# Four edits ahead of the feed-forward part of a spectral block: a shorter chain to the first angles, gathers behind the last rstd, shared PSUM tiles for the last stage-1 casts, another order of the first pairs

## Chip, cores, metric

One core of one Trainium2 chip. The metric is the device time of one execution in microseconds (us), median of several runs. The profile gives in addition the span, from the first to the last instruction of the core (some 1.8 us less than the time).

## What is computed

```python
def reference(A_x, A_w_r, A_w_i, B_x, B_w1, B_b1, B_w2, B_b2):
    # x: (1, 2048, 512) bf16; w_r, w_i: (2048, 257); w1: (512, 1792); w2: (1792, 512)
    x = A_x
    h  = x + irfft2(rfft2(layernorm(x)) * (w_r + 1j * w_i))
    h2 = h + (relu(layernorm(h) @ w1 + b1) ** 2) @ w2 + b2
    return h2
```

The two-dimensional Fourier transforms are done as matmuls with tables of sines and cosines, which the kernel makes itself from integer angles. The 2048 rows are split into 16 groups of 128 for the first part.

## The kernel before: the parts concerned

The rows of x arrive in five loads. The third of them holds groups 4 to 7:

```python
CH = ((0, 2), (2, 4), (4, 8), (8, 12), (12, 16))
for a, b in CH:
    ld.append(nc.sync.dma_start(xs[:, a:b, :], xv[:, a:b, :]))
```

VectorE makes the first angles (fiE) out of the partition number, and then starts on the statistics of the layer norm:

```python
nc.vector.tensor_single_scalar(pI[:, 1:2], pI[:, 0:1], 3, ALU.arith_shift_right)
nc.vector.tensor_single_scalar(pI[:, 2:3], pI[:, 0:1], 7, ALU.bitwise_and)
nc.vector.tensor_copy(pF[:], pI[:, 0:3])
nc.vector.tensor_scalar(cols[:, 2:3], pF[:, 2:3], 512.0, None, ALU.mult)
nc.vector.tensor_scalar(cols[:, 3:4], pF[:, 1:2], 32.0, cols[:, 2:3], ALU.mult, ALU.add)
nc.vector.tensor_scalar(cols[:, 6:7], cols[:, 3:4], 16.0, None, ALU.mult)
nc.vector.tensor_scalar(ck1[:], idx1[:], cols[:, 3:4], None, ALU.mult)
nc.vector.scalar_tensor_tensor(fiE[0]..., idx2..., cols[:, 6:7], ck1..., ALU.mult, ALU.add)
```

Stage 1 multiplies two row groups at a time. The layer norm's rstd (one over the standard deviation of a row) is "folded" into the table (KFr = KF times rstd), TensorE multiplies, and the result in PSUM is cast to Bt. PSUM is one pool of four slots of two banks each (`bufs=4`, 1024 floats). The last four groups are "split": each half of a result has a slot of its own, so that ScalarE casts one half and VectorE the other:

```python
def stage1(g0, n=0, split=False, ...):
    if split:
        two = [mm_tile("p1a"), mm_tile("p1b")]
        pts = [pt[:, 0:512] for pt in two]
    else:
        pt = mm_tile("p1")
        pts = [pt[:, 0:512], pt[:, 512:1024]]
    ...                                     # 8 matmuls
    if split:
        for t, cph in ((0, nc.scalar.copy), (1, nc.vector.tensor_copy)):
            cph(dst[:, 2 * t:2 * t + 2], pts[t]...)
```

Then come eight pairs of frequencies. For each, stage 2 gives U, stage 3 gives A and B (AB, cast by ScalarE), VectorE makes X out of AB and multiplies X by the weights (mA, mB), combines them into Z and M, and stage 4 transforms back:

```python
stage2_one(0, 0, nc.vector.tensor_copy, 3)
stage2_one(0, 1, nc.scalar.copy)
stage2_one(1, 0, nc.scalar.copy)
...
stage3(0)
stage2_one(1, 1, nc.scalar.copy)
stage2(2)
stage3(1)
stage3(2)
for pr in range(9):
    ...                                     # stage 2 and 3 of later pairs, stage 4 of the last one
    spectral(pr)                            # VectorE
```

The weights of the rows above the middle are gathered by GpSimd, half of them before the last rstd, which GpSimd makes too.

## Time and profile before

| | before |
|---|---|
| time, median of 3 runs | 172.66 us (172.52 to 172.68) |
| span of the profile | 170.8 us |
| busy in the span: TensorE, VectorE, ScalarE, GpSimd | 92%, 72%, 62%, 22% |
| first angles (fiE) start | 2.48 |
| last two folds start | 17.47 |
| first multiply by the weights (mA) starts | 23.62 |
| last M of the spectral part ends | 48.00 |
| from there to the end of the span | 122.8 |

The last five rows are positions in us from the start of the span, read off VectorE's timeline. Everything that was edited lies before 48.0. TensorE's 92% is mostly the feed-forward part behind that point. The question is therefore not who is busiest but what sets the pace in each stretch of the first 48 us.

### The profile page before, as it was taken

How to read it: one execution, taken by the hardware profiler on the slowest of the kernel's cores; microseconds unless marked ns; L12 is line 12 of the kernel's file. 1: busy time of each engine (PE TensorE's matmuls, PEld its weight loads, DVE VectorE, ACT ScalarE, POOL GpSimd, SP SyncE). 2: the span in 40 equal slices, each digit the busy share in tenths (PEclk: the TensorE clock that was granted, in tenths of full speed). 3: DMA queues.
4: the chain of work that ended last, by engine and by line, in shares of the span. 5: the costliest groups of instructions: out<-in, count | busy, mean ns of one | idle time of the engine just before them, and what ended most of it. 6: DMA issues, size and time to landing. Idle time of an engine off the chain costs nothing.

```text
span 170.8 us, 2709 instructions
## 1 busy us (share of the span) xinstructions
PE 157.6 (92%) x967; PEld 92.4 (54%) x981; DVE 123.6 (72%) x287; ACT 106.3 (62%) x188; POOL 36.7 (22%) x63
## 2 busy tenths in 40 slices
PE   3988797999989899899999999999999999999992
PEld 1455565887854774456445444544544454556461
DVE  6998678979956698668997577498567577578320
ACT  3999785898976772288653677245387434478200
POOL 7788900000000003134000235000034200025000
PEclk9999999999999999999999999999999999999999
DMA  5994999992000000100000100000100001010011
GB/s 165 326 281 83 223 152 272 387 241 26 0 0 0 4 0 2 55 12 0 0 31 31 35 0 2 0 31 31 35 30 0 0 31 33 25 38 0 0 60 34
DMA packets 12621, 11.42 MB, mean 67 GB/s; under 512 B 6976, under 2 KB 11072, under 8 KB 12608
## 3 DMA queue, kind: packets, MB, share of 16 engines
q1 hardware_dynamic: 12448, 10.33, 22.6%
q0 software_dynamic: 160, 0.92, 1.9%
q8 instruction: 7, 0.11, 0.3%
q14 instruction: 6, 0.05, 0.1%
HBM read 8.01 MB, written 2.10 MB: 59 GB/s over the span
## 4 chain that ended last, share of the span: by engine, by line
PE 72%; DVE 16%; ACT 5%; issue 2%; POOL 2%; DVEq 0%; POOLq 0%; ACTq 0%
PE ph L688 29%; PE po L721 25%; DVE st L215 3%; PE p L542 3%; PE p L344 3%; ACT U L361 2%; PE po L709 2%; PE p L643 2%; PE p L587 1%; PE idle L259 1%; POOL rs L222 1%; DVE KFr L226 1%; DVE mA L419 1%; ACT X L391 1%; DVE mB L419 1%
## 5 line engine op out<-in xcount | busy, mean ns | idle before, releaser
L688 PE MATMUL ph<-UT,W 128*128 128x384 bf16 (+2 forms) x278 | 49.8, 336 | 1.6 <-DVE UT L774 0.6
L691 ACT ACTIVATE rl<-ph,b1f 128x384 bf16<-128x384 f32 (+2 forms) x70 | 41.5, 602 | 13.7 <-PE ph L688 10.6
L721 PE MATMUL po<-W,act 128*128 128x512 bf16 x203 | 48.1, 379 | 0.4
L692 DVE TENSOR_TENSOR act<-rl 128x384 bf16<-128x384 bf16 (+2 forms) x70 | 34.2, 514 | 15.4 <-ACT rl L691 14.9
L688 PEld LDWEIGHTS <-W 128*128 128x128 bf16 x280 | 27.3, 98 | 22.9 <-issue 2.1
L695 POOL TENSOR_TENSOR hb<-hs,b2b 128x512 f32<-128x512 bf16 x16 | 18.4, 1153 | 98.2 <-DVE act L692 98.2
L721 PEld LDWEIGHTS <-act 128*128 128x128 bf16 x210 | 20.4, 98 | 21.8
L725 DVE TENSOR_TENSOR ot<-po,hb 128x512 bf16<-128x512 f32 x15 | 10.3, 688 | 9.3 <-PE po L721 8.0
L591 DVE SCALAR_TENSOR_TENSOR hs<-p,xs 128x512 bf16<-128x512 f32 x15 | 10.3, 684 | 1.2 <-PE p L587 0.9
L259 PE MATMUL p<-ones 128*128 128x512 bf16 x22 | 8.1, 516 | 2.9 <-POOL ones L152 2.9
L546 ACT COPY od<-p 128x256 f32<-128x256 f32 x14 | 5.1, 370 | 7.9 <-PE p L542 7.9
L647 ACT COPY UT<-p 128x768 bf16<-128x768 bf16 (+1 forms) x4 | 3.6, 906 | 9.4 <-PE p L643 9.4
L542 PE MATMUL p<-GI,T 128*128 128x256 bf16 x56 | 8.2, 272 | 0.4 <-DVE hs L591 0.2
L259 PEld LDWEIGHTS <-ones 128*128 128x128 bf16 x40 | 4.4, 112 | 7.6 <-POOL ones L152 2.9
L602 ACT ACTIVATE junk<-hs 128x512 bf16<-128x512 bf16 x6 | 3.8, 630 | 7.6 <-DVE hs L591 7.6
L344 PE MATMUL p<-GF,Bt 128*128 128x256 bf16 x64 | 8.3, 273 | 0.0
L577 DVE TENSOR_TENSOR R<-p,od 128x256 bf16<-128x256 f32 x15 | 6.2, 415 | 2.4 <-ACT od L561 1.3
L215 DVE BATCH_NORM_STATS2 st<-xs 128x6 f32<-128x512 bf16 x12 | 7.8, 676 | 0.0
L542 PEld LDWEIGHTS <-T 128*128 128x128 bf16 x56 | 5.4, 97 | 3.5 <-issue 1.2
L473 ACT CAST T<-p 128x1024 bf16<-128x1024 f32 x7 | 7.2, 1025 | 0.0
L344 PEld LDWEIGHTS <-Bt 128*128 128x128 bf16 x64 | 6.1, 98 | 1.4 <-DVE Bt L251 0.4
L605 DVE BATCH_NORM_STATS2 st<-hs 128x6 f32<-128x512 bf16 x9 | 6.3, 695 | 0.3
(177 smaller groups left out, 226.0 us busy)
## 6 DMA issues: line engine op xcount, KB each, us to landing
W<-in_B_w_dram SPq DMA_DIRECT2D x2, 1792.0 KB, 10.3
out_dram<-ot SPq DMA_DIRECT2D x15, 128.0 KB, 1.8
xs<-in_A_x_dram SPq DMA_DIRECT2D x3, 512.0 KB, 6.5
WB<-in_A_w_r_dram SPq DMA_DIRECT2D x1, 578.2 KB, 6.0
WB<-in_A_w_i_dram SPq DMA_DIRECT2D x1, 578.2 KB, 7.2
xs<-in_A_x_dram SPq DMA_DIRECT2D x2, 256.0 KB, 3.3
b2b<-in_B_b_dram SPq DMA_DIRECT2D x1, 128.0 KB, 8.7
out_dram<-ot SPq DMA_DIRECT2D x2, 64.0 KB, 1.9
```

Source lines behind the costliest of these rows:

```text
L215: nc.vector.bn_stats(st[:], xs[:, g, :])
L259: nc.tensor.matmul(o, lhsT=ones[:, 0:P], rhs=ones[:], start=True, stop=True)
L344: nc.tensor.matmul(puv[:, :, e, :], lhsT=Bt[:, 2 * t + 1 - e, 2 * pr + q, :], rhs=GFv[:, t, :, e, :], start=(t == 0), stop=(t == 1))
L473: nc.scalar.copy(dst, src[0])
L542: nc.tensor.matmul(pe[:, 256 - 256 * e:512 - 256 * e], lhsT=T2[:, lt, g].rearrange("p q s -> p (q s)"), rhs=GI[:, lt, :], start=(r == 0), ...
L591: nc.vector.scalar_tensor_tensor(hs[:, g, :], Ys.pop(g)[:], WSC, xs[:, g, :], ALU.mult, ALU.add)
L688: nc.tensor.matmul(ph[:, 0:n], lhsT=W1[:, d, bass.ts(f, P)], rhs=UT[:, d, 0:n], start=(d == 0), stop=(d == ND - 1))
L691: nc.scalar.activation(rl[:, 0:n], ph[:, 0:n], ACT.Relu, bias=b1f[:, f:f + 1], scale=1.0)
L692: sq = nc.vector.tensor_tensor(act[:, f, 0:n], rl[:, 0:n], rl[:, 0:n], ALU.mult)
L695: add = nc.gpsimd.tensor_tensor(hb[:, g, :], hs[:, g, :], b2b[:], ALU.add)
L721: nc.tensor.matmul(po[:], lhsT=act[:, f, bass.ts(i, P)], rhs=W2[:, f, :], start=(f == 0), stop=(f == NF - 1))
L725: nc.vector.tensor_tensor(ot[:], po[:], hb[:, g, :], ALU.add)
```

## The change

The intent is in four parts. (1) The first angles come from three integer steps and do not need the cast to float. (2) Both gathers are issued after the last rstd. (3) The last stage-1 results use one slot each again, but are still cast in halves by two engines; before this they needed two slots each, and a matmul waited for a slot. A small cosine table moves behind the casts on ScalarE. (4) The first two pairs are ordered anew: the matmuls of the first U start on the half of Bt that is ready first, stage 3 of pair 1 goes before stage 2 of pair 2, and the first multiply and the second pair's cast come in halves.

```diff
--- before.py
+++ after.py
@@ -123,7 +123,7 @@
 
         nc.scalar.activation(dst, fi.bitcast(I16)[:, ::2], ACT.Sin, scale=SIN_SCALE)
 
-    pI = tab.tile([P, 4], I32, name="pI")
+    pI = tab.tile([P, 6], I32, name="pI")
     pF = tab.tile([P, 3], FP32, name="pF")
     rowA = tab.tile([P, 16, 8], I32, name="rowA")
     subc = tab.tile([P, 16, 8], I32, name="subc")
@@ -169,15 +169,16 @@
     nc.gpsimd.affine_select(out=ident[:], in_=ident[:], compare_op=ALU.not_equal,
                             fill=1.0, base=0, pattern=[[-1, P]], channel_multiplier=1)
 
+
+    nc.vector.tensor_scalar(pI[:, 4:5], pI[:, 0:1], 7, 9, ALU.bitwise_and, ALU.logical_shift_left)
+    nc.vector.tensor_scalar(pI[:, 5:6], pI[:, 0:1], 3, 5, ALU.logical_shift_right, ALU.logical_shift_left)
     nc.vector.tensor_single_scalar(pI[:, 1:2], pI[:, 0:1], 3, ALU.arith_shift_right)
+    nc.vector.tensor_tensor(cols[:, 3:4], pI[:, 4:5], pI[:, 5:6], ALU.add)
     nc.vector.tensor_single_scalar(pI[:, 2:3], pI[:, 0:1], 7, ALU.bitwise_and)
+
+    nc.vector.tensor_scalar(ck1[:], idx1[:], cols[:, 3:4], None, ALU.mult)
+    nc.vector.tensor_scalar(cols[:, 6:7], cols[:, 3:4], 16.0, None, ALU.mult)
     nc.vector.tensor_copy(pF[:], pI[:, 0:3])
-
-    nc.vector.tensor_scalar(cols[:, 2:3], pF[:, 2:3], 512.0, None, ALU.mult)
-    nc.vector.tensor_scalar(cols[:, 3:4], pF[:, 1:2], 32.0, cols[:, 2:3], ALU.mult, ALU.add)
-    nc.vector.tensor_scalar(cols[:, 6:7], cols[:, 3:4], 16.0, None, ALU.mult)
-
-    nc.vector.tensor_scalar(ck1[:], idx1[:], cols[:, 3:4], None, ALU.mult)
     nc.vector.scalar_tensor_tensor(fiE[0][:].rearrange("p (a b) -> p a b", a=9),
                                    idx2[:].unsqueeze(1).to_broadcast([P, 9, P]), cols[:, 6:7],
                                    ck1[:].unsqueeze(2).to_broadcast([P, 9, P]), ALU.mult, ALU.add)
@@ -226,17 +227,11 @@
             last = eng.tensor_scalar(KFr[:, g, :], KF[:], rs1[:, g:g + 1], None, ALU.mult)
         return last
 
-    def stage1(g0, n=0, split=False, pre=None, cp=nc.scalar.copy):
-        if split:
-            two = [mm_tile("p1a"), mm_tile("p1b")]
-            pts = [pt[:, 0:512] for pt in two]
-        else:
-            pt = mm_tile("p1")
-            pts = [pt[:, 0:512], pt[:, 512:1024]]
+    def stage1(g0, n=0, halves=False):
+        pt = mm_tile("p1")
+        pts = [pt[:, 0:512], pt[:, 512:1024]]
         pvs = [o.rearrange("p (e i c) -> p e i c", e=2, i=2) for o in pts]
         warm(pts[0], n)
-        if pre:
-            pre(two[0][:, 512:1024].bitcast(BF16))
         for t in range(2):
             for i in range(2):
                 g = g0 + i
@@ -246,12 +241,11 @@
                 nc.tensor.matmul(o, lhsT=xs[:, g, 256 + P * t:256 + P * t + P],
                                  rhs=KFr[:, g, :].rearrange("p (e c) -> p e c", e=2), start=False, stop=True)
         dst = Bt[:].rearrange("p e q (g s) -> p e g q s", s=8)[:, :, g0:g0 + 2]
-        if split:
-            for t, cph in ((0, nc.scalar.copy), (1, nc.vector.tensor_copy)):
-                cph(dst[:, 2 * t:2 * t + 2], pts[t].rearrange("p (e i q s) -> p e i q s", e=2, i=2, q=16))
-            return two[0][:, 512:1024].bitcast(BF16)
+        if halves:
+            for t, cp in ((0, nc.scalar.copy), (1, nc.vector.tensor_copy)):
+                cp(dst[:, 2 * t:2 * t + 2], pts[t].rearrange("p (e i q s) -> p e i q s", e=2, i=2, q=16))
         else:
-            cp(dst, pt[:].rearrange("p (e i q s) -> p e i q s", e=4, i=2, q=16))
+            nc.scalar.copy(dst, pt[:].rearrange("p (e i q s) -> p e i q s", e=4, i=2, q=16))
 
     def warm(o, n):
 
@@ -289,30 +283,29 @@
     ln1_fold(2, 6)
     stage1(2, 6)
     stage1(4)
-    table_c(slice(0, 9, 8))
     ln1_stats(10, 12)
     ln1_fold(6, 10)
     nc.gpsimd.tensor_scalar(fiG[:, 512:768], idxL[:, 0:256], cols[:, 1:2], float(QT), ALU.mult, ALU.add)
     ln1_rstd(10, 14)
     nc.gpsimd.tensor_scalar(fiG[:, 768:1024], idxL[:, 256:512], cols[:, 1:2], float(HT), ALU.mult, ALU.add)
-    gathers = [w_reversed(0)]
     stage1(6, 2)
-    sin_of(GF[:].rearrange("p t c -> p (t c)"), fiG[:])
     ln1_stats(14)
     ln1_fold(10, 12)
     stage1(8)
+    sin_of(GF[:].rearrange("p t c -> p (t c)"), fiG[:])
     ln1_stats(15)
     nc.vector.tensor_scalar(rs1[:, 14:16], mv1[:, 14:16, 1], EPS, None, ALU.add)
     nc.gpsimd.tensor_tensor(rs1[:, 14:16], rs1[:, 14:16], mhalf[:, 0:2], ALU.pow)
     ln1_fold(12, 14)
-    gathers.append(w_reversed(1))
+    gathers = [w_reversed(i) for i in range(2)]
     ln1_fold(14, 16)
     stage1(10)
-    stage1(12, split=True)
+    stage1(12, halves=True)
 
     nc.vector.tensor_scalar(GF[:, :, 255:256], GF[:, :, 255:256], 0.5, None, ALU.mult)
+    stage1(14, halves=True)
     nc.vector.tensor_scalar(EF[:, 2, :, :], EF[:, 0, :, :], -1.0, None, ALU.mult)
-    stage1(14, split=True)
+    table_c(slice(0, 9, 8))
     turned(EI[:, :, 0, :], EF[:, 0, :, :])
     turned(KI[:].unsqueeze(1), KF[:, 0:P])
     for k in (0, 8):
@@ -343,6 +336,19 @@
             for t in range(2):
                 nc.tensor.matmul(puv[:, :, e, :], lhsT=Bt[:, 2 * t + 1 - e, 2 * pr + q, :], rhs=GFv[:, t, :, e, :],
                                  start=(t == 0), stop=(t == 1))
+
+    def stage2_first():
+
+        os = [mm_tile(f"p2{q}")[:, 0:512] for q in range(2)]
+        warm(os[0], 3)
+        for t in range(2):
+            for q in range(2):
+                puv = os[q].rearrange("p (r e j) -> p r e j", r=2, e=2)
+                for e in range(2):
+                    nc.tensor.matmul(puv[:, :, e, :], lhsT=Bt[:, 2 * t + 1 - e, q, :], rhs=GFv[:, t, :, e, :],
+                                     start=(t == 0 and e == 0), stop=(t == 1 and e == 1))
+        for q, cp in ((0, nc.vector.tensor_copy), (1, nc.scalar.copy)):
+            cp(Us[0][:, q].rearrange("p (r j e) -> p r j e", r=2, e=2), os[q].rearrange("p (r e j) -> p r j e", r=2, e=2))
 
     def new_u(pr):
         Us[pr] = fwd.tile([P, 2, 512], BF16, tag="U", bufs=3, name="U")
@@ -372,7 +378,7 @@
                 nc.tensor.matmul(o, lhsT=C, rhs=U[:, u, :], start=True, stop=False)
                 nc.tensor.matmul(o[:, 0:256], lhsT=Sp, rhs=U[:, u, 256:512], start=False, stop=False)
                 nc.tensor.matmul(o[:, 256:512], lhsT=Sn, rhs=U[:, u, 0:256], start=False, stop=True)
-            for u, cp in ((0, nc.scalar.copy), (1, nc.vector.tensor_copy)):
+            for u, cp in ((0, nc.vector.tensor_copy), (1, nc.scalar.copy)):
                 cp(X[:, u].rearrange("p r c -> p (r c)"), pxs[u][:, 0:512])
         elif pr in ON_PE:
             C, Sp, Sn, Cm = EF[:, 1, pr, :], EF[:, 0, pr, :], EF[:, 2, pr, :], Cn[:, pr - 1, :]
@@ -397,7 +403,8 @@
             nc.tensor.matmul(px[:, 512:1024], lhsT=C, rhs=U[:, 1, :], start=True, stop=False)
             nc.tensor.matmul(px[:, 512:1024], lhsT=Sp, rhs=U[:, 0, :], start=False, stop=True)
             ABs[pr] = AB = fwd.tile([P, 2, 2, 256], BF16, tag="AB", bufs=3, name="AB")
-            nc.scalar.copy(AB[:].rearrange("p u r c -> p (u r c)"), px[:])
+            for u in ((0, 1) if pr == 1 else (slice(0, 2),)):
+                nc.scalar.copy(AB[:, u], px[:].rearrange("p (u r c) -> p u r c", u=2, r=2)[:, u])
 
     def butterfly(pr):
 
@@ -415,8 +422,10 @@
         mA = fwd.tile([P, 2, 2, 256], BF16, tag="mA", bufs=2, name="mA")
         mB = fwd.tile([P, 2, 2, 256], BF16, tag="mB", bufs=2, name="mB")
         step = 16 - 2 * pr if pr else 8
-        for m, w in ((mA, WB[0]), (mB, WB[1])):
-            nc.vector.tensor_tensor(m[:], X[:], w[:, pr:pr + step + 1:step, 1:Df].unsqueeze(2).to_broadcast([P, 2, 2, 256]), ALU.mult)
+        for u in ((0, 1) if pr == 0 else (slice(0, 2),)):
+            for m, w in ((mA, WB[0]), (mB, WB[1])):
+                nc.vector.tensor_tensor(m[:, u], X[:, u], w[:, pr:pr + step + 1:step, 1:Df].unsqueeze(2)
+                                        .to_broadcast([P, 2, 2, 256])[:, u], ALU.mult)
         Zs[pr] = Z = fwd.tile([P, 2, 2, 256], BF16, tag="Z", bufs=2, name="Z")
         ABs.pop(pr, None)
         if pr > 0:
@@ -474,9 +483,9 @@
 
     new_u(0)
     new_u(1)
-    stage2_one(0, 0, nc.vector.tensor_copy, 3)
-    stage2_one(0, 1, nc.scalar.copy)
-    stage2_one(1, 0, nc.scalar.copy)
+    stage2_first()
+    stage2_one(1, 0, nc.vector.tensor_copy)
+    stage2_one(1, 1, nc.scalar.copy)
     cos_negs()
     for k, (dst, src) in enumerate(((W1[:], B_w1.rearrange("(c p) f -> p c f", p=P)),
                                     (W2[:], B_w2.rearrange("(i p) d -> p i d", p=P)),
@@ -487,15 +496,15 @@
             for ga in gathers:
                 after(load, ga, "the rows of W first")
     stage3(0)
-    stage2_one(1, 1, nc.scalar.copy)
+    stage3(1)
     stage2(2)
-    stage3(1)
-    stage3(2)
     for pr in range(9):
         if pr == 1:
             stage3(3)
         if pr + 3 < 8:
             stage2(pr + 3)
+        if pr == 0:
+            stage3(2)
         if 1 < pr and pr + 2 < 8:
             stage3(pr + 2)
         if pr == 7:
```

## The prediction

> **What bounds the kernel now.** I read the chain that ended last first (where is time on the path at all?), then a table of busy time by stage, then the timelines of VectorE, ScalarE and GpSimd over the first 50 us, then waits and DMA landings. All edits lie before the feed-forward part, so I want to know which engine sets the pace in each stretch of that first part. The table by stage (columns: stretch, length, busy us and count of each engine, clock, DMA share):
>
> ```profile
> 0.00:3.90 3.90, 1.03 (x3) 0.43 (x4) 2.65 (x9) 1.28 (x1) 3.07 (x19) 1.00 0.47 147
> 3.90:18.60 14.70, 12.63 (x75) 7.48 (x73) 13.65 (x46) 14.29 (x28) 12.12 (x21) 1.00 0.84 234
> 18.60:23.60 5.00, 4.86 (x37) 3.62 (x38) 2.82 (x7) 3.63 (x7) 2.75 (x8) 1.00 1.04 148
> 23.60:48.00 24.40, 22.50 (x180) 16.90 (x181) 22.34 (x50) 20.81 (x23) 0.37 (x1) 1.00 0.67 182
> 56.60:170.80 114.20, 109.09 (x627) 59.53 (x636) 77.71 (x167) 60.75 (x119) 18.40 (x16) 1.00 0.06 19
> ```
>
> From 3.9 to 18.6 us (layer norm and stage 1) VectorE (third pair, 13.65 of 14.70) and ScalarE (fourth, 14.29) are both full. From 18.6 to 23.6 nobody but TensorE is busy, and some of that is warming matmuls: a chain of dependent small steps. From 23.6 to 48.0 VectorE is busy 22.34 of 24.40. After 56.6 TensorE has 109 of 114 us, and nothing there is edited: I let it move as a block. The beginning and end of stage 1, from the chain of waits:
>
> ```profile
> 0.99 0.15 DVE pI L172
> 1.24 0.36 DVE pF L174
> 1.62 0.16 DVE cols L176
> 1.81 0.23 DVE cols L177
> 2.48 1.42 DVE fiE L181
> ...
> 16.70 0.74 POOL rs L306
> 17.47 0.48 DVE KFr L226 x2
> 17.95 0.66 DVE Bt L251
> 18.66 0.27 PE p1a L244
> ```
>
> First angles (fiE) start at 2.48 after a string of one-column operations. At the other end, the last rstd begins on GpSimd at 16.70 though its input was ready at 16.34: a gather issued before it holds GpSimd from 15.44 to 16.67. The last stage-1 matmuls (18.66) then wait for a VectorE cast that only empties the PSUM slot they were given; their folds were done by 17.95. The waits of 15 to 48 us show the rest:
>
> ```profile
> DVE X L409 <- ACT AB L400: 1.5, 3, 0.9
> PE p L395 <- ACT U L361: 1.1, 1, 1.1
> PE p1a L244 <- DVE Bt L251: 0.8, 1, 0.8
> DVE KFr L226 <- POOL rs L306: 0.7, 1, 0.7
> DVE Bt L251 <- PE p1b L246: 0.7, 1, 0.7
> ```
>
> The first row is all that VectorE loses once it has entered the spectral stage (at 26.1, 31.2 and 38.4).
>
> **What the Trainium skill says.** "Perfetto Trace Analysis", section Optimizing Scalar/DVE Operations: every VectorE or ScalarE operation carries a fixed access overhead, yet breaking instructions up may let dependent work finish sooner. The trace agrees: 1024-element multiplies follow each other every 0.605 us and 512-element ones every 0.34, so a split costs 0.075 us per piece. "PSUM — Partial Sum Buffer", section Terms: two engines must not touch one bank and quadrant at once. So the halves of a slot may be cast by ScalarE and VectorE together only because each half is its own 512-float bank; no wait follows from sharing a slot. "DMA: Bandwidth & Descriptors", section Issuing engines are not separate DMA queues: gathers and transposes end up on the same 16 engines. The trace agrees: the transpose issued at 19.07, beside the gathers, lands at 24.88 (5.8 us), the one issued alone at 23.83 after 3.1 us.
>
> **The change part by part.**
>
> *First angles.* Before, shift, mask, a cast (0.36), three one-column float steps, ck, fiE. After, two integer operations, one add and ck lead to fiE; the cast leaves the dependency but still stands ahead of fiE on the engine. With 0.07 us between independent small operations and 0.15 to 0.2 for each dependent one (rows above), fiE starts at about 1.9 instead of 2.48: −0.55. But x arrives late: chunks land at 3.61, 4.98, 6.42, 8.64 and 9.93 us. The first statistics move from 4.64 to 4.05, but the fourth one (row group 4) now waits for 6.42 against 6.65 before. What survives on VectorE is about −0.2. ScalarE's third row sum starts at 8.66, just after the chunk at 8.64, so ScalarE gains nothing here.
>
> *Gathers behind the last rstd.* VectorE reaches the input of that rstd at 16.14 (16.34 − 0.2). GpSimd is then free, so rstd runs 16.18 to 16.92 and the last folds start at 16.95 instead of 17.47: −0.52 including the −0.2.
>
> *ScalarE order.* The small cosine table (0.32) leaves the row of stage-1 casts. The sine for GF only swaps places. ScalarE is full from 8.66: casts at 0.91 each from 12.50, GF 0.96, then the two 0.5 half-casts, which end at 19.05 instead of 19.84.
>
> *Single slots.* Matmuls of groups 12 and 13 start at 16.64 and end at 17.5; 14 and 15 follow at once and end at 18.37 (8 × 0.109), no longer waiting for 18.66. VectorE's last half-cast runs 18.57 to 19.26 instead of 19.73 to 20.42: −1.16. Nearly 0.8 of this is the slot wait, 0.35 the gather.
>
> *First pairs.* The ordering t-first starts on ScalarE's half at 19.1, finishes U of q=0 at 19.95; VectorE casts it 19.98 to 20.67 (before 21.01). The tables (0.32 + 0.90) now occupy ScalarE from 19.05 to 20.26, so its first U cast starts at 20.26 rather than 20.17: not critical. U(1,0) on VectorE 20.6 to 21.25, negations to 21.55, the first X half 21.55 to 22.24 by VectorE, the other by ScalarE. The first multiply starts at 22.27 instead of 23.62: −1.35. Four half-multiplies take 1.36 against 1.21: +0.15, but the first no longer waits for both halves. Z then starts at 23.70 (24.95 − 1.25).
>
> *Stage 3 of pair 1 before stage 2 of pair 2.* Its AB comes in halves, ready at about 23.6, and VectorE wants it at 24.4. The 0.38 wait at 26.09 goes: the second pair's multiply starts at 25.2 instead of 26.89 (−1.7). Stage 3 of pair 2 follows U(2) at 24.6 and ends at 26.4; stage 3 of pair 3 starts there instead of 29.12 (−2.7). From then TensorE is dense in both versions, so AB(3) is ready at 28.4 where VectorE wants it at 29.2 (0.24 wait gone) and AB(5) at 35.5 where VectorE wants it at 35.4 (0.87 wait down to 0.1). VectorE alone could be 2.9 ahead at 38; TensorE and then ScalarE, which is full from 40.65 to 49.77 (X6, casts, GI, table load), are 2.7 ahead. The later one counts: −2.7.
>
> Sum: −1.35 (first multiply) + 0.15 − 0.05 (rest of the entry) − 1.45 (waits for AB) = −2.7 on the path, if all later waits keep their places. I take off 0.2 for small slips: **170.2 us**.
>
> **The rivals.**
>
> *The gathers land late.* Second gather: issue now 18.1 to 19.2, landing at +6.3 as before (17.62 to 23.96) is 24.5; VectorE multiplies by its rows at about 25.8. Against: 1.3 us of slack. For: its transfers now run beside three or four transposes. If it landed 1 us later than that, half of the gain in waits would go: 170.7.
>
> *The transposes become the wait.* The small cosine table ends at 19.4 instead of 14.6, so the two small transposes and all behind them in SP's order slide by about 2.5 us. Stage 4 of pair 0 (30.85 before, 28.15 now) needs the transposed −sine, which I put at 26.5 to 27.5. A slip of 1 us would stall TensorE and take about 1 us back: 171.0. This is my main worry. The feed-forward weights, 2.5 us later, land at 41 against a need at 53: harmless.
>
> *Stage 1 is already bound elsewhere.* If ScalarE's row of casts does not shorten (say, the GF sine still lies in its way), stage 1 ends at 19.6 and the gain falls by 0.4: 170.6. For: ScalarE is 14.29 of 14.70 busy there. Against: the cosine table is really taken out of it.
>
> *It goes better.* If x's landing does not eat the front's 0.55 and ScalarE's end closes up, 169.3.
>
> **Range and chances.** The edits reach only the first 48 us, where I can name 2.06 us of VectorE idle in the spectral stage and about 1.4 before it, so over 3.45 us (2%, under 169.2) needs all of it and more. Range 169.1 to 171.4. Faster by over 2%: 0.09; within 2%: 0.90; slower: 0.01, since nothing new lies on the feed-forward part, which is two thirds of the time.
>
> **What would show it.** Angles starting near 1.9 and statistic of group 4 waiting for x; rstd on GpSimd with no gather ahead of it; no wait of stage-1 matmuls on a VectorE cast; first spectral multiply near 22.3; stage 3 of pair 3 near 26.4; no VectorE wait for AB over 0.2. The feed-forward stretch must keep its 114 us. I am wrong if VectorE waits for the gathered rows, TensorE for transposes, or if the last VectorE M of the stage, ending at 48.0 before, does not end near 45.3.

## The result and the profile after

| | before | after |
|---|---|---|
| time, median | 172.67 us (172.52 to 172.93, 4 runs) | 170.64 us (170.44 to 171.22, 4 runs) |
| ratio | | 0.9886, 95% interval 0.9859 to 0.9914 |
| span | 170.8 | 168.7 |
| first angles | 2.48 | 2.01 |
| last two folds | 17.47 | 16.98 |
| first cast of U | 21.01 | 20.49 |
| first multiply | 23.62 | 22.96 |
| last M ends | 48.00 | 45.96 |
| from there to the end | 122.80 | 122.74 |

Ratios here and below are the mean time of one kernel's fast runs over that of the other's in the same rounds, so they are not quite the ratio of the medians quoted beside them. The kernel became 1.1% faster: 2.0 us, where 2.5 were predicted.

The table of busy time by stage of the changed kernel, with its columns as in the prediction and its stretches cut at the changed kernel's own positions:

```profile
0.00:3.90 3.90, 1.07 (x3) 0.44 (x4) 2.64 (x11) 1.72 (x2) 3.07 (x19) 1.00 0.53 134
3.90:18.60 14.70, 13.70 (x84) 8.44 (x83) 12.63 (x43) 14.01 (x28) 10.99 (x20) 1.00 0.73 210
18.60:23.00 4.40, 3.99 (x29) 2.50 (x27) 4.22 (x9) 3.30 (x6) 3.86 (x8) 1.00 0.76 215
23.00:45.96 22.96, 22.28 (x184) 16.99 (x182) 22.23 (x52) 20.53 (x24) 0.22 (x1) 1.00 0.75 202
54.50:168.70 114.20, 109.56 (x636) 59.58 (x636) 77.64 (x167) 60.77 (x119) 18.37 (x16) 1.00 0.06 19
```

The last row is the same 114.2 us of feed-forward as before: that part moved as a block. The fourth row is the spectral stretch, 22.96 us long in place of 24.38; VectorE is busy 22.23 of it, as much as before, so what went is its waiting. The third row, where a chain of small steps ran, is 4.4 us instead of 5.0.

The chain of waits of the changed kernel, up to the first multiply (start, length, what):

```profile
2.11 6.49 DMA xs<-in_A_x_dram
...
8.62 0.73 ACT junk L208 x2
...
12.56 3.63 ACT Bt L248 x4
16.19 0.96 ACT GF L124
17.15 0.90 ACT Bt L248
18.05 0.50 ACT Bt L246
...
18.57 0.69 DVE Bt L246
19.26 0.44 DVE GF L305
...
19.75 0.92 PE p L348 x7
```

This answers to the second block of the prediction, and it looks quite different. GpSimd's rstd and VectorE's folds are no longer in it, nor is the angle chain. It starts with the fourth load of x (groups 8 to 11), goes on with ScalarE's own row of sums and casts, and at the end has a cast by ScalarE (18.05), *then* a cast by VectorE (18.57), then the halving of a column of GF (19.26), then the first matmuls of stage 2 at 19.75. The two casts were meant to run side by side. The chain follows one releaser per step, and two engines that are equally late look like one; so I do not conclude from it that VectorE has time to spare.

The waits between 15 and 48 us of the changed kernel (total, times, longest):

```profile
DVE Bt L246 <- ACT Bt L246: 1.1, 1, 1.1
...
DVE KFr L227 <- POOL rs L298: 0.4, 1, 0.4
...
PE p L348 <- DVE GF L305: 0.4, 1, 0.4
...
DVE X L416 <- ACT AB L407: 0.2, 1, 0.2
```

The wait of the stage-1 matmuls for a VectorE cast (0.8 before) is gone, and so are two of the three waits for AB: 0.2 is left of 1.5. The wait for rstd is 0.4 instead of 0.7. But the first line is new: VectorE waits 1.1 us for a ScalarE instruction, the cast of the *other half* of the same PSUM tile.

### The profile page after: what moved, and what is told of

Same layout as the page of the kernel before. It is cut to its first block, busy times and chain, and to the rows that moved or that the text cites. A ratio compares the mean times of both kernels' runs of the same rounds, so it can differ in the third digit from the quotient of the medians.

```text
span 168.7 us, 2729 instructions
## 1 busy us (share of the span) xinstructions
PE 158.1 (94%) x981; PEld 92.4 (55%) x981; DVE 123.8 (73%) x291; ACT 105.8 (63%) x188; POOL 36.5 (22%) x63
## 4 chain that ended last, share of the span: by engine, by line
PE 73%; ACT 9%; DVE 9%; DMA 4%; issue 2%; SPq 1%; ACTq 0%; DVEq 0%
PE ph L697 29%; PE po L730 25%; DMA xs<-in_A_x_dram 4%; ACT Bt L248 3%; PE p L551 3%; PE p L337 3%; PE po L718 2%; ACT junk L208 2%; PE p L652 2%; PE p L596 1%; PE idle L253 1%; DVE mA L427 1%; DVE mB L427 1%; DVE Z L433 1%; DVE Z L434 1%
## 5 line engine op out<-in xcount | busy, mean ns | idle before, releaser
L730 PE MATMUL po<-W,act 128*128 128x512 bf16 x210 | 49.1, 379 | 0.0
L239 PE MATMUL p<-KFr,xs 128*128 128x256 bf16 x32 | 7.4, 275 | 1.0 <-DVE KFr L227 1.0
L241 PE MATMUL p<-KFr,xs 128*128 128x256 bf16 x32 | 7.3, 272 | 0.0
L337 PE MATMUL p<-GF,Bt 128*128 128x256 bf16 x56 | 7.1, 272 | 0.0
```

The source lines that it names most:

```text
L239: nc.tensor.matmul(o, lhsT=xs[:, g, P * t:P * t + P], rhs=KFr[:, g, 0:P].unsqueeze(1).to_broadcast([P, 2, P]), start=True, stop=False)
L337: nc.tensor.matmul(puv[:, :, e, :], lhsT=Bt[:, 2 * t + 1 - e, 2 * pr + q, :], rhs=GFv[:, t, :, e, :], start=(t == 0), stop=(t == 1))
L730: nc.tensor.matmul(po[:], lhsT=act[:, f, bass.ts(i, P)], rhs=W2[:, f, :], start=(f == 0), stop=(f == NF - 1))
```

## Experiments

Most of the front moves as a block with one load, as will be seen, so the profiles are compared from a fixed point: **A**, the start of the aggregates that follow the statistic of group 4. I give three distances: A to the last folds, the folds to the first cast of U, and A to the end of the span. (The first and second profile of a kernel agree in the last to 0.2 us, although their spans differ by up to 0.8. r8 and r9 order the loads or the statistics otherwise and are left out. The span is printed to 0.1 us, so the last column is good to 0.05.)

| profile | third load of x lands | A | A to folds | folds to U | first mA to last M | A to end |
|---|---|---|---|---|---|---|
| before | 6.42 | 7.22 | 10.25 | 3.54 | 24.38 | 163.58 |
| r12_before_again | 6.77 | 7.40 | 10.25 | 3.54 | 24.38 | 163.50 |
| after | 6.41 | 7.04 | 9.94 | 3.51 | 23.00 | 161.66 |
| r1_after_again | 7.39 | 8.02 | 9.94 | 3.25 | 23.20 | 161.48 |
| r2_two_slots | 6.85 | 7.48 | 9.94 | 3.34 | 22.93 | 161.52 |
| r3_whole_casts | 7.14 | 7.77 | 9.94 | 3.39 | 23.17 | 161.53 |
| r4_gf_early | 6.99 | 7.62 | 9.95 | 3.25 | 23.17 | 161.48 |
| r5_four_slots | 6.98 | 7.62 | 9.94 | 3.09 | 23.18 | 161.28 |
| r6_old_pairs | 6.50 | 7.14 | 9.94 | 3.36 | 24.40 | 163.06 |
| r7_gather_back | 6.45 | 7.08 | 10.26 | 3.61 | 23.21 | 162.02 |
| r10_old_front | 6.94 | 7.58 | 9.94 | 3.25 | 23.17 | 161.42 |
| r11_pairs_only | 6.71 | 7.35 | 10.24 | 3.64 | 23.19 | 162.05 |

A is not the only fixed point. ScalarE's row of sums and casts starts anew on groups 8 to 11, the fourth load of x, which landed anywhere from 8.05 to 9.21 us in the 13 profiles with undivided loads (9.44 in r8). In the changed kernel ScalarE's first half-cast (groups 12 and 13) comes at the later of two marks: 10.68 to 10.69 us after A (r1, r2, r4, r6, r10), or 9.32 us after this load landed, with ScalarE full from there on (after, r5, r7, and r8, in which it landed 1.55, 1.59, 1.82 and 2.79 after A). So the first profile of the changed kernel is late by this load, 10.87 from A to the half-cast, and that is most of the 0.2 us by which it differs from r1 in the last column.

My theory after the first comparison: the order of the first pairs brings most of the gain; the slot part is nearly given back because the halves of one tile are cast one after the other; the front is hidden behind a load of x. Rivals: the gathers held VectorE's small operation on GF (0.52 us in the profile after); the gain comes from stage 1 and the new order only passes it on; the front's half microsecond is really on the path.

### r1_after_again: the changed kernel once more

No edit.

> The changed kernel as it is, to have its time on the same chip and in the same rounds as the three variants. Expected: about 0.9886 of the kernel before (170.6 us), last M of the spectral stage ending near 45.96 us, VectorE's cast of the second half of groups 12 and 13 starting at 18.57, right after ScalarE's cast of the first half.

Measured: 171.17 us (170.65 to 171.26), ratio 0.9899 [0.9881, 0.9916]. This profile is 0.8 us longer than the first one of the same program, and VectorE's timeline says why. The statistic of group 4 in the first profile of the changed kernel (start, length, engine, line, operation, its operands, and in brackets the idle time before it with what ended it):

```profile
6.43 0.69 DVE L216 BATCH_NORM_STATS2 st<-xs 128x6 f32<-128x512 bf16 x1 [0.29 <-DMA xs<-in_A_x_dram]
```

The same row in this second profile:

```profile
7.41 0.69 DVE L216 BATCH_NORM_STATS2 st<-xs 128x6 f32<-128x512 bf16 x1 [1.27 <-DMA xs<-in_A_x_dram]
```

The third load of x landed 0.98 us later (7.39 against 6.41), and the statistic started 0.98 later. From A to the folds the two profiles agree to 0.01 us, and from A to the end to 0.2. So most of the difference between these two spans is set at the very start, by when 512 KB arrive. And the operation on GF took 0.16 us in this profile, not 0.52.

### r2_two_slots: the halves of the last tiles in tiles of their own

```diff
-        pt = mm_tile("p1")
-        pts = [pt[:, 0:512], pt[:, 512:1024]]
+        if halves:
+            pts = [mm_tile(f"p1{h}")[:, 0:512] for h in "ab"]
+        else:
+            pt = mm_tile("p1")
+            pts = [pt[:, 0:512], pt[:, 512:1024]]
```

> The changed kernel with the halves of the last two stage-1 tiles back in PSUM tiles of their own. Theory 1 (halves of one tile are cast one after the other, because the program makes VectorE's read wait for ScalarE's read of the same tile): VectorE's first half-cast starts near 17.55 instead of 18.57, its last ends near 19.6 instead of 19.98, U of q=0 is cast from about 20.05 instead of 20.49, and the kernel gains 0.4 us on the changed one. Rival (the slot wait of before was the dear thing and single slots cured it): the last matmuls of stage 1 wait for a slot again, stage 1 ends later than 19.98, and the kernel loses 0.4 to 0.8 us. Rival (ScalarE's row of casts, from the landing of x at 8.6 on, sets the end of stage 1): nothing moves by over 0.1 us.

Measured: 170.81 us (170.42 to 171.03), ratio 0.9883 [0.9865, 0.9901]: the same time. VectorE's last steps of stage 1 in the changed kernel's first profile:

```profile
16.98 0.48 DVE L227 TENSOR_SCALAR KFr<-KF,rs 128x256 bf16<-128x256 bf16 x2 [0.44 <-POOL rs L298]
18.57 0.69 DVE L246 CAST Bt<-p 128x512 bf16<-128x512 f32 x1 [1.10 <-ACT Bt L246]
19.18 0.52 DVE L305 TENSOR_SCALAR GF<-GF 128x2 bf16<-128x2 bf16 x1
19.30 0.68 DVE L246 CAST Bt<-p 128x512 bf16<-128x512 f32 x1
...
20.49 0.69 DVE L351 CAST U<-p 128x512 bf16<-128x512 f32 x1
```

The first half-cast (18.57) waits 1.10 us for ScalarE's. In this run:

```profile
18.00 0.69 DVE L249 CAST Bt<-p1b 128x512 bf16<-128x512 f32 x1
...
19.38 0.69 DVE L249 CAST Bt<-p1b 128x512 bf16<-128x512 f32 x1 [0.60 <-PE p1b L244]
```

The first half-cast starts 0.58 after the folds (17.42), with no wait for ScalarE; but now the second waits 0.60 for its matmuls, and TensorE's timeline shows what these wait for:

```profile
18.75 0.27 PE L242 MATMUL p1b<-KFr,xs 128*128 128x256 bf16 x1 [0.34 <-DVE Bt L249]
```

That is the wait for a slot of the kernel before. One wait is exchanged for the other. It settles where the 1.10 comes from: it goes when the halves get tiles of their own, although the same matmuls and casts are done. In the program, too, VectorE's cast waits on a semaphore that ScalarE's cast raises; nothing in the data asks for that, since both only read the PSUM tile. They also write two different parts of Bt; that they do in r2 too, where there is no such wait, so Bt is not the reason.

### r3_whole_casts: no halves at all

Groups 12 and 13 are cast whole by VectorE, 14 and 15 whole by ScalarE:

```diff
-    stage1(12, halves=True)
+    stage1(12, cast=nc.vector.tensor_copy)
...
-    stage1(14, halves=True)
+    stage1(14)
```

> The changed kernel with single slots, but groups 12 and 13 cast whole by VectorE and groups 14 and 15 whole by ScalarE, so that no two engines read one tile. Theory 1: VectorE's cast runs from 17.55 to 18.8, ScalarE's from 18.4 to 19.35, the second stage starts near 19.4 and U of q=0 is cast from 20.2 instead of 20.49: 0.25 us gained. If the halving of one column of GF is held up by GpSimd's gather (issued 18.66 to 19.61), as its 0.52 us instead of 0.16 suggests, it ends near 19.65 and nothing is gained. The ScalarE rival: no change either, since ScalarE then carries the last cast.

Measured: 170.84 us (170.58 to 171.15), ratio 0.9887 [0.9869, 0.9905]; U comes 3.39 after the folds. Halves that run one after the other are worth nothing over whole casts: the kernel's splitting brought no gain in this place.

### r4_gf_early: the operation on GF ahead of the half-casts

```diff
     stage1(10)
-    stage1(12, halves=True)
-
     nc.vector.tensor_scalar(GF[:, :, 255:256], GF[:, :, 255:256], 0.5, None, ALU.mult)
+    stage1(12, halves=True)
     stage1(14, halves=True)
```

> The changed kernel with the halving of GF's column moved ahead of VectorE's cast of groups 12 and 13, into the 1.1 us in which VectorE waits. Theory 1 alone: the last half-cast moves up by 0.1, from 19.98 to 19.88, and the first half of stage 2's matmuls runs before it, so U of q=0 is cast from about 20.27 instead of 20.49: 0.2 us gained. Theory 2 (a one-source VectorE operation waits while GpSimd issues a gather): the halving, now beside the first gather (issued 17.14 to 18.37), takes until 18.4, about 0.9 us. Against theory 2: it takes 0.16 us, right after the last fold.

Measured: 170.65 us (170.48 to 170.97), ratio 0.9877 [0.9861, 0.9894]. The operation took 0.17 us at 17.96, while GpSimd was issuing a gather (17.72 to 18.95). So the rival "the gather holds it" falls as a rule. "SBUF — State Buffer", section Who interferes with whom, says that such a VectorE operation can take a port pair that GpSimd also needs, and that the loser blocks for a whole instruction. Both lengths occur here, 0.52 (after) and 0.16 (r1), beside the issue of the same gather. What lengthened the one I could not settle. It cost little: from VectorE's first half-cast to the first cast of U it is 1.92 us in that profile (18.57 to 20.49) and 1.86 in r1, so hardly 0.1 of the 0.36 went through.

### r5_four_slots: a tile for each half

All four half-casts get tiles of their own, allocated together, and the warming matmuls (their result is not read; they only keep TensorE running), which took a slot, write into one of them:

```diff
     stage1(10)
-    stage1(12, halves=True)
+    four = [mm_tile(f"p1{h}") for h in "abcd"]
+    stage1(12, halves=four[0:2])
...
-    stage1(14, halves=True)
+    stage1(14, halves=four[2:4])
...
-        warm(os[0], 3)
+        warm(four[1][:, 512:1024], 3)
```

> The changed kernel with the four halves of the last two stage-1 tiles in four PSUM slots, held so that none takes over a slot whose cast is still to come. The two-slots run showed VectorE's first half-cast freed (0.58 us after the start of the last folds instead of 1.4 to 1.6) but the last matmuls waiting for that very cast, so nothing was gained. Here neither wait is left. Theory 1 (the cast order in one tile, or else the slot wait, costs the step): VectorE's last half-cast ends about 2.3 us after the start of the last folds (2.63 with two slots, 2.74 and 3.0 with single slots), U of q=0 is cast 2.9 us after it (3.25 to 3.5 with single slots), and the kernel is 0.4 us faster than the changed one, 0.987 or lower against before. Rival (ScalarE's row sets the end): VectorE's last half-cast is early but U of q=0 stays at 3.2 to 3.5 us after the last folds.

Measured: 170.64 us (170.58 to 170.70), ratio 0.9864 [0.9846, 0.9883]. VectorE at the end of stage 1:

```profile
18.14 0.69 DVE L249 CAST Bt<-p1b 128x512 bf16<-128x512 f32 x1
...
19.35 0.69 DVE L249 CAST Bt<-p1d 128x512 bf16<-128x512 f32 x1 [0.43 <-PE p1d L244]
```

No wait for ScalarE, and the last cast waits only 0.43 for its matmuls. A wait for a slot is not quite gone, though: the fourth tile takes the slot of groups 10 and 11, and its matmuls wait for ScalarE's cast of those:

```profile
18.71 0.27 PE L242 MATMUL p1d<-KFr,xs 128*128 128x256 bf16 x1 [0.17 <-ACT Bt L251]
```

U comes 3.09 after the folds, and A to the end is 161.28 against 161.48 in r1. So the two waits under test together hide 0.2 us, where 0.4 was expected; r9, which has no wait for a slot at all, comes to the same. By time alone this is not told from the changed kernel.

### r6_old_pairs: the changed kernel without the new order

The order of the first pairs, the halves of the first multiply and of AB, and the engines of the first U and X casts are as before; the other three parts stay:

```diff
-    stage2_first()
-    stage2_one(1, 0, nc.vector.tensor_copy)
-    stage2_one(1, 1, nc.scalar.copy)
+    stage2_one(0, 0, nc.vector.tensor_copy, 3)
+    stage2_one(0, 1, nc.scalar.copy)
+    stage2_one(1, 0, nc.scalar.copy)
...
-    stage3(1)
+    stage2_one(1, 1, nc.scalar.copy)
     stage2(2)
+    stage3(1)
+    stage3(2)
```

> The changed kernel with the first pairs as before: stage 2 of pair 0 by halves of q, old order of stages 2 and 3, whole multiplies, AB of pair 1 in one cast. My account says that this part alone carries the gain inside the spectral stage: from the first multiply to the end of the last M 24.4 us as before instead of 23.0, VectorE waiting three times for AB, 1.5 us in all, and the first multiply 0.2 to 0.3 us later. Expected 172.3 us, 0.998 of before. Rival (the gain comes from the earlier stage 1, and the waits for AB would have gone with it): below 171.3, 0.992.

Measured: 172.30 us (171.98 to 172.75), ratio 0.9968 [0.9952, 0.9985]. The waits of 15 to 48 us in this run:

```profile
DVE X L416 <- ACT AB L407: 1.5, 3, 0.9
...
PE p L401 <- ACT U L367: 1.1, 1, 1.1
```

The three waits for AB are back at their old sizes (0.39, 0.23 and 0.88 at 25.5, 30.7 and 37.8), and TensorE's wait of 1.1 for a U with them. From A to the end it takes 163.06, 1.58 more than r1. The three other parts alone bring 0.3% of the 1.1%.

### r7_gather_back: the first gather before the last rstd again

```diff
+    gathers = [w_reversed(0)]
     stage1(6, 2)
...
-    gathers = [w_reversed(i) for i in range(2)]
+    gathers.append(w_reversed(1))
```

> The changed kernel with the first gather issued ahead of the last rstd again. The last folds should start 10.8 us after the fourth statistic instead of 10.55, and 0.25 to 0.3 us be lost: 0.9905 to 0.991 of before. If ScalarE's row of casts is what sets the end of stage 1, nothing is lost, since the last folds then have that much room.

Measured: 170.94 us (170.76 to 170.95), ratio 0.9879 [0.9864, 0.9895]. The last folds wait longer for GpSimd, as in the kernel before:

```profile
17.34 0.48 DVE L227 TENSOR_SCALAR KFr<-KF,rs 128x256 bf16<-128x256 bf16 x2 [0.71 <-POOL rs L299]
```

A to the folds is 10.26 in place of 9.94. A to the end is 162.02, 0.36 more than in the first profile of the changed kernel and 0.54 more than in r1, but that is not shown to be the gather's doing. The fourth load of x landed at 8.90 here, 1.82 after A, and ScalarE is full from there to its half-casts:

```profile
8.93 0.63 ACT L208 ACTIVATE junk<-xs 128x512 bf16<-128x512 bf16 x1 [0.65 <-DMA xs<-in_A_x_dram]
...
18.23 1.12 ACT L246 CAST Bt<-p 128x512 bf16<-128x512 f32 x2
```

VectorE's first half-cast waits 1.07 for ScalarE's. From that landing to the end it is 160.2 us here and 160.1 in the first profile. So this profile shows the second case of the expectation: ScalarE's row sets the end of stage 1, and the later folds have room. The runs that were timed show no loss either: their ratio lies between those of r1 and r4, which are the changed kernel in all but one small operation. Where VectorE's row sets the pace the gather can be worth the 0.31 of the folds, and no run here measures how much of it reaches the time.

### r8_split_load: the third load of x in two

```diff
-    CH = ((0, 2), (2, 4), (4, 8), (8, 12), (12, 16))
+    CH = ((0, 2), (2, 4), (4, 6), (6, 8), (8, 12), (12, 16))
...
-            after(w, ld[2], "the rows of x first")
+            after(w, ld[3], "the rows of x first")
```

> The changed kernel with the third load of x (row groups 4 to 7, 512 KB) as two loads of 256 KB. In five profiles of the changed kernel and its variants the fourth statistic waits for that load, landing between 6.41 and 7.39 us, and everything on VectorE up to the last folds follows at a fixed distance of 10.55 us. Theory 3 (this landing has taken the place of the chain to the first angles): group 4 lands 0.4 to 0.8 us earlier, the wait is at most 0.3 us, the last folds start by 16.9 us, and the kernel gains 0.3 us on the changed one's mean and spreads less. Rival: the extra issue (0.46 us on the queue) delays the later loads, ScalarE's third row sum starts at 9.0 instead of 8.6, and nothing is gained.

Measured: 170.66 us (170.57 to 171.29), ratio 0.9868 [0.9851, 0.9884]. Groups 4 and 5 landed at 5.44, a microsecond earlier, but groups 8 to 11 at 9.44, where all other profiles have 8.1 to 9.2, and VectorE lost there what it had won: the last folds stand at 17.50. The wait moved to the next load. No gain is shown.

### r9_best: everything that helped, and two small moves

r5, with the sine for GF moved behind ScalarE's cast of groups 10 and 11, and the negation of EF moved into VectorE's wait for x:

```diff
-    ln1_stats(2, 4)
+    ln1_stats(2)
+    nc.vector.tensor_scalar(EF[:, 2, :, :], EF[:, 0, :, :], -1.0, None, ALU.mult)
+    ln1_stats(4)
...
-    sin_of(GF[:].rearrange("p t c -> p (t c)"), fiG[:])
     ln1_stats(15)
...
     stage1(10)
+    sin_of(GF[:].rearrange("p t c -> p (t c)"), fiG[:])
```

> Built on r5_four_slots (after, with four tiles of their own for the four half-casts): the halving for the sine of GF moves to just after ScalarE's cast of groups 10 and 11, and the negation of EF moves on VectorE from behind the last half-casts to between the statistics of groups 2 and 4, where VectorE waits for the third load of x. Theory (what is left between the last fold and the first U tile is the in-order row of ScalarE and VectorE): no wait for a slot, last half-cast ends 2.0 us after the fold (r5: 2.48), first U tile 2.9 after it (r5: 3.09), 0.1 to 0.3 us below r5, so about 170.3 us and a ratio of 0.985 where the x load lands as in r5. Rival A (the row's other links take the room): as r5, 0.986. Rival B (the negation holds GpSimd's first rstd or the next statistic): the fold comes 10.7 or more after statistic 4 in place of 10.55, and the time is that of r5 or longer.

Measured: 170.48 us (170.26 to 171.06), ratio 0.9863 [0.9842, 0.9884]. No wait for a slot is left and VectorE's last half-cast ends 2.15 after the folds (2.48 in r5), but U comes 3.05 after them, as in r5 (3.09). The reason is ScalarE's row:

```profile
17.02 1.01 ACT L251 CAST Bt<-p 128x1024 bf16<-128x1024 f32 x1
17.93 1.06 ACT L124 ACTIVATE GF<-fiG 128x1024 bf16<-128x1024 int16 x1
18.89 0.58 ACT L249 CAST Bt<-p1a 128x512 bf16<-128x512 f32 x1
19.35 0.60 ACT L249 CAST Bt<-p1c 128x512 bf16<-128x512 f32 x1
```

Its last half-cast ends at 19.95, 2.00 after the folds (17.95), as in r5 (2.07), with no idle time in between; the matmuls of the first U, which start on ScalarE's half, come at 20.14. That is rival A of the expectation: another row takes the room. The lowest median, but not told apart from the changed kernel, whose interval reaches down to 0.9859.

### r10_old_front: the angle chain as before

The first part of the diff undone, all else as changed.

```diff
-    nc.vector.tensor_scalar(pI[:, 4:5], pI[:, 0:1], 7, 9, ALU.bitwise_and, ALU.logical_shift_left)
-    nc.vector.tensor_scalar(pI[:, 5:6], pI[:, 0:1], 3, 5, ALU.logical_shift_right, ALU.logical_shift_left)
...
-    nc.vector.tensor_tensor(cols[:, 3:4], pI[:, 4:5], pI[:, 5:6], ALU.add)
...
+    nc.vector.tensor_copy(pF[:], pI[:, 0:3])
...
+    nc.vector.tensor_scalar(cols[:, 2:3], pF[:, 2:3], 512.0, None, ALU.mult)
+    nc.vector.tensor_scalar(cols[:, 3:4], pF[:, 1:2], 32.0, cols[:, 2:3], ALU.mult, ALU.add)
```

> The changed kernel with only the front undone: the angle chain is that of the kernel before. Theory (the third load of x sets when statistic 4 starts, so the chain ahead of it is mostly hidden): first float angle copy at 2.5 us as before (after: 2.0), statistic 4 at the later of 6.65 and its load, every later position at its fixed distance (last fold 10.55 after it), and the time as r1_after_again within 0.25 us: 170.6 to 171.2, ratio 0.988 to 0.990. Rival (the chain's 0.47 us is on the path): statistic 4 half a microsecond later than in r1 at the same landing, 171.2 to 171.7, ratio 0.991 to 0.994.

Measured: 170.87 us (170.43 to 171.25), ratio 0.9891 [0.9871, 0.9911]. fiE starts at 2.48 again, and nothing follows from it: the load landed at 6.94, A is at 7.58, and A to the end is 161.42. Half a microsecond off the chain is worth nothing when the load lands later than the chain ends.

### r11_pairs_only: the kernel before with the new order alone

The fourth part of the diff alone.

> The kernel before with only the other order of the first pairs. Theory (this part carries most of the gain): first multiply to end of the last one 23.0 to 23.3 us in place of 24.38, no wait of 0.87 for AB left, 1.2 to 1.5 us faster than before: 171.3 to 171.7 us, ratio 0.991 to 0.993; the first U tile at least 3.5 after the last fold, as before. Rival (the parts need each other: the gain of the order hangs on the earlier end of stage 1): 24 or more between those two points, ratio above 0.995.

Measured: 171.30 us (171.12 to 172.01), ratio 0.9921 [0.9900, 0.9942]. First multiply to last M: 23.19. A to the end is 162.05, 1.49 less than before (mean of 163.58 and 163.50). The order does not need the other parts. At the end of stage 1 nothing has changed: VectorE's last half-cast waits the same 0.69 for its matmul as in the kernel before, and the first U comes 3.64 after the folds.

### r12_before_again: a second profile of the kernel before

> The kernel before once more, for a second profile of it. Theory (landing of x sets the front, in this kernel too): statistic 4 at the later of about 6.65 and the landing of the third load of x, the last fold 10.82 after it, first U tile 3.5 after that, first multiply to the end of the last 24.4; if x lands at 7.4 as in r1 the profile's span is 171.5 or so, if at 6.4 it is 170.8. Rival (the front is bound by its own chain): statistic 4 at 6.65 whenever x lands.

Measured: 172.72 us (2 runs), ratio 0.9997. VectorE's statistics of groups 2 and 4 in the first profile of the kernel before, merged into one row by the timeline:

```profile
6.04 1.25 DVE L215 BATCH_NORM_STATS2 st<-xs 128x6 f32<-128x512 bf16 x2
```

And in this one:

```profile
6.04 1.45 DVE L215 BATCH_NORM_STATS2 st<-xs 128x6 f32<-128x512 bf16 x2
```

The start is the same and the pair takes 0.20 longer: a wait for the load, which landed at 6.77 instead of 6.42, is hidden inside a merged row. In the first profile the fourth statistic could start at about 6.65; here it waited, and A moved by 0.18. So the theory holds for this kernel too: the load sets the front as soon as it lands late. The distance from A to the folds is 10.25 in both profiles, and the span is 0.1 longer.

## Why the prediction was right or wrong

**The first angles: mechanism right, size too large.** fiE starts at 2.01 (predicted 1.9) and the statistic of group 4 waits for x, as said. I left 0.2 on VectorE. In 13 profiles with that load in one piece (all but r8) it lands between 6.41 and 7.39, mean 6.84. In the ones with the changed chain A comes 0.63 after the landing (0.75 in r9, which has an operation more there); with the old chain A can't come before 7.22, which answers to a landing at 6.59. Only four of the 13 land earlier than that, by 0.09 to 0.18; averaged over all 13, the shorter chain is worth 0.04 us (an estimate from these numbers). The first profile is the luckiest case: it has the earliest landing of all, and A did move by 0.18 there. r10 agrees: nothing lost. The landing also goes with the spread of the changed kernel's runs, as far as two profiled ones show: 170.52 us at a landing of 6.41, 171.26 at 7.39.

**Gathers behind the last rstd: right.** The gather's share is 0.31 on VectorE's row (A to folds 10.25 and 9.94), shown by r7 and r11, where it comes back. How much of it reaches the time is open. That the folds, predicted at 16.95, came at 16.98 is partly luck: in other profiles with the same distance from A they stand as late as 17.96, with the load.

**Single slots: the step that failed.** "So the halves of a slot may be cast by ScalarE and VectorE together only because each half is its own 512-float bank; no wait follows from sharing a slot." The wait for a slot did go, as predicted. But a wait did follow: the halves of one tile were cast one after the other, 1.1 us for VectorE in the first profile. I reasoned about the banks; the program kept order by tile here, even between two reads. I had VectorE's last half-cast at 18.57 to 19.26; 18.57 is when its *first* one started, and the last ran from 19.30. The first U, predicted 3.03 after the folds, came 3.51 (after) and 3.25 (r1) after them. VectorE's last half-cast ends 2.99 (after) and 2.77 (r1) after the folds, in place of 2.95 before. So of nearly 0.8 for the slot 0 to 0.2 came. r2 shows the old wait returning where the new one goes; r5 removes both and gains 0.2. The rest of the room is taken by ScalarE's row, which ends 2.0 to 2.1 after the folds in r5 and r9; in r5 and in the first profile that row is late by the fourth load of x.

**ScalarE order: right in its times.** The half-casts on ScalarE end at 19.02 (predicted 19.05), the tables behind them at 20.18 (predicted 20.26). ScalarE is full from the fourth load on, as said; but that the load landed at 8.60, where 8.64 was assumed, is luck: 8.05 to 9.21 was possible.

**First pairs: right.** Between the first multiply and the last M 1.35 were predicted to go (1.45 of waits less 0.15 for the split, with 0.05 of entry); 1.38 went in the first profile, 1.18 in r1. Undone alone it costs 1.58 from A to the end, and done alone it brings 1.49, part of it ahead of the first multiply (first U to first multiply: 2.61 before, 2.28 in r11). One of the three waits, predicted at 0.1, is 0.23 to 0.43 in all profiles with the new order but r2, which has none; so the sign "no VectorE wait for AB over 0.2" failed. (With 0.1 left of that wait, the prediction's own terms 0.38, 0.24 and 0.77 make 1.39 and not 1.45.) Stage 3 of pair 3 came at 27.09, not near 26.4.

**The sum.** From A to the end it is 163.54 before and 161.48 in r1: 2.06 us, of which the order has 1.5 to 1.6. That leaves some 0.5 for the gather, shared slots and ScalarE's order together, where 0.8 stood in the prediction for the slot alone; how it divides is not measured (the folds come 0.31 earlier, which the gather explains). By time, the order alone gives 0.79% and the rest without it 0.32%, together 1.11% of the whole 1.14%: the parts add up, within intervals of some 0.2% each way. The last M ended at 45.96, not near 45.3, so by its own sign the prediction was 0.66 off in the first profile: 0.5 of that at the first U (20.49 for 19.98), the rest up to the first multiply (22.96 for 22.27). That the total of 170.2 still lay close to 170.64 owes something to the 0.2 taken off for slips and to the order carrying most of the gain; the slot term itself was wrong.

**The rivals.** Gathers too late: refuted; they land at 22.03 and 24.22, and the multiply by their rows starts at 25.89 unheld. Transposes as the wait: refuted; the transposed −sine lands at 25.80, and stage 4 of pair 0 starts at 28.82 by its own order. Stage 1 bound elsewhere: it holds, not because ScalarE's row failed to shorten, but because VectorE was tied to it, and because that row starts with a load that can land late. That rival's 170.6 is what came, for another reason than the one given.

**Open:** why the operation on GF took 0.52 us once (and 0.33 in r7) and 0.16 or 0.17 in all other profiles; and how much of the gather's part survives in the time. The prediction's 3.1 us for a transpose "issued alone" at 23.83 is not quite that: one issued at 20.75 was still under way until 25.68.

## What to carry to other kernels

When two engines are to empty one buffer together, give each of them a tile of its own, or look in the trace whether the second waits for the first: here the program's order went by tile, not by what is read. Before shortening a chain, look at how the transfer next to it varies over several profiles: if it lands later than the chain ends in most of them, the chain is already hidden. And measure parts from a point behind such a transfer; distances from there repeated to 0.1 or 0.2 us, where the times of four runs spread by 0.8. But look first whether another engine's row hangs on another transfer: here ScalarE's did, and in r7 it looked like the cost of a gather.

## What the Trainium skill lacked or had wrong

- "PSUM — Partial Sum Buffer", section PSUM bank collisions raise a hardware error, tells to guard by bank and quadrant. Two reads of two different banks of one tile were nevertheless ordered by the program here: 1.10 us (after) and 0.91 us (r1) of wait on VectorE, none in r2 and r5 with a tile for each half. No page says that the guard may come out coarser than the bank.
- "DMA: Bandwidth & Descriptors", section 🔬 Latency and other measured facts, gives an average and a high-load latency but no spread for one transfer under a kernel's own load. The third of five loads of x, 512 KB, landed anywhere from 6.41 to 7.39 us in 13 profiles of nearly the same front, the fourth from 8.05 to 9.21.
- "SBUF — State Buffer", section Who interferes with whom: its rule of an exclusive lock, which goes to whoever issues first, would explain the 0.52 us of a two-column VectorE operation beside the issue of a gather. But the same operation beside the same issue took 0.16 us (r1), and 0.17 us beside the other gather's (r4), though GpSimd's row had begun first in all three. So the rule cannot be read off whole rows of a gather's issue.
- "Perfetto Trace Analysis", section Optimizing Scalar/DVE Operations, puts VectorE's overhead on SBUF at about 60 ns an operation. In the trace before, 1024-element operations follow each other every 0.605 us and 512-element ones every 0.34, which makes it 75 ns (2 × 0.34 less 0.605).
